# A retention layer with a gated feed-forward layer: tiles of one chunk of all batch entries, and a down projection as seven products of halves

## The chip, the cores and the metric

The kernel runs on one core of one Trainium2 chip. A core has TensorE (PE in the profile; its weight loads are shown apart, as PEld), VectorE (DVE), ScalarE (ACT), GpSimd (POOL), and SyncE (SP), which here only issues DMAs. PSUM, which TensorE writes to, has eight banks; SBUF holds everything else. The metric is the time of the launch on the device in microseconds (us); the figure for the kernel before is a median of three runs.

## The reference

Two layers follow one another. The first is a recurrence over 768 positions for 4 batch entries (B) and 8 heads (H) of size 64 (D), in float32:

```python
gamma = 1.0 - 2.0 ** (-5.0 - np.arange(H))
scale = 1.0 / np.sqrt(D)
for t in range(S):
    state = gamma[None, :, None, None] * state + np.einsum('bhd,bhe->bhde', k[:, :, t], v[:, :, t])
    y[:, :, t] = scale * np.einsum('bhd,bhde->bhe', q[:, :, t], state)
```

Its output, reordered to x of (B*S, H*D) = (3072, 512), goes through a gated feed-forward layer with 1536 hidden columns:

```python
gate = 1.0 / (1.0 + np.exp(-(x @ w_gate)))
val = x @ w_val
return (gate * val @ w_out).astype(np.float32)
```

## The kernel before

**Chunks.** The recurrence is computed by chunks of 128 positions: inside a chunk as masked products (scores of k against q, a causal mask, then a product with v), and across chunks through a state of 64x64 for each head. There are 24 chunks, six for each batch entry, and they are worked through batch entry by batch entry. The decay is put in by tables: v is multiplied by a table on the way in (`scale_v`, `tabv`), and the output by another on the way out (`y_out`, `taby`). So k and q are used as they are loaded, and a state must pass from a chunk to the next.

**Steps of a chunk.** `load_kq` and `load_v` bring a chunk's k and q as bf16 and v as float32 (three DMAs that GpSimd issues; those of chunk 0 are issued by SyncE). k and q are then transposed: for chunks 0 to 11 on TensorE (`transposes`, `transposes_early`, evicted by ScalarE), from chunk 12 on by DMA (`xbar`, on SyncE's queue). `scores` fills two PSUM banks, `masks` moves them to SBUF on VectorE, `inter` multiplies the state of the chunks before (`zbd`) with q, `intra` adds the chunk's own part, `y_out` writes the result, times its table, on VectorE into `xT`, the input of the feed-forward layer. `state`, `state_sum` and `casts` carry the state on. From chunk 4 on, two chunks at a time go through `block`.

**Tiles of the feed-forward layer.** Four chunks make one tile of 512 tokens, six tiles in all. For each of twelve groups of 128 hidden columns, `up` makes eight matmuls of 128x512 into two banks; ScalarE takes the sigmoid of one (`gs`), VectorE multiplies it with the other into `hT`. `up_columns` does the same for columns that become ready later. `down` takes twelve matmuls of 128x512 for each 128 tokens (48 for a tile), ScalarE copies the bank out, SyncE stores it. The last 128 tokens go through `last_down`, in three pieces of 256, 128 and 128 columns.

**Order.** The order on every engine is written out by hand (`manual_schedule`): a list of groups for each tile, in which a plan puts the attention steps between `up` and `down` groups. Each engine works its list in order. PSUM tiles are one bank each, seven banks in a pool named `ff` in the profile, and one for the state (`z`). Since TensorE works in order, a matmul whose input or bank isn't ready holds back all that follow. `keep_on` issues matmuls without a use in the first microseconds.

Of the kernel before, what the change touches and what calls it, by code (L numbers as in the profile page):

```python
# [17 lines left out]
def kernel(  # L18
# [15 lines left out]
    NCH = S // C  # L34
    NP = H // 2
    KT = D_MODEL // 128
    NFF = D_FF // 128
    scale = 1.0 / math.sqrt(D)
# [5 lines left out]
    ld = ctx.enter_context(tc.tile_pool(name="ld", bufs=12))  # L44
# [5 lines left out]

    NG = B * NCH
    NT = N_TOK // 512
    XBAR = 12
    qn, kn, vf = {}, {}, {}

    def src(x, g):
        b, c = divmod(g, NCH)
        return x[b, :, c * C:(c + 1) * C, :].rearrange("h s d -> s h d")

    def load_v(g, eng):  # L60
        vf[g] = ld.tile([C, H, D], F32, tag="vf", name="vf", bufs=8)
        eng.dma_start(out=vf[g], in_=src(v, g))  # L62

    def load_kq(g):
        kn[g] = ld.tile([C, H, D], BF16, tag="kn", name="kn")
        qn[g] = ld.tile([C, H, D], BF16, tag="qn", name="qn")
        nc.gpsimd.dma_start(out=kn[g], in_=src(k, g))  # L67
        nc.gpsimd.dma_start(out=qn[g], in_=src(q, g))  # L68

    def load_chunk(g):  # L70
        load_kq(g)
        load_v(g, nc.gpsimd)
# [16 lines left out]
    kf = const.tile([C, H, D], F32, name="kf")  # L89
    qf = const.tile([C, H, D], F32, name="qf")  # L90
    nc.sync.dma_start(out=kf, in_=src(k, 0))
    nc.sync.dma_start(out=qf, in_=src(q, 0))
    nc.scalar.preload_act_table(AX.Exp)
    load_v(0, nc.sync)
    tokv = const.tile([128, NCH], I32, name="tokv")
    nc.gpsimd.iota(tokv, pattern=[[C, NCH]], base=0, channel_multiplier=1)
    ident = const.tile([128, 128], BF16, name="ident")
    make_identity(nc, ident)
    toky = const.tile([128, 384], I32, name="toky")
    nc.gpsimd.iota(toky, pattern=[[1, 384]], base=0, channel_multiplier=0)  # L100
    load_chunk(1)
# [4 lines left out]
    load_chunk(2)  # L106

    tabv = const.tile([128, NCH, H], F32, name="tabv")
    for h in range(H):
        nc.scalar.activation(tabv[:, :, h], tokv, AX.Exp, scale=-lg[h])  # L110
    lgp = const.tile([128, NP], F32, name="lgp")
    lsc = const.tile([128, 1], F32, name="lsc")
    nc.vector.memset(lsc, math.log(scale))
    for p in range(NP):
        nc.vector.memset(lgp[0:D, p:p + 1], lg[2 * p])
        nc.vector.memset(lgp[D:128, p:p + 1], lg[2 * p + 1])
    gup = const.tile([128, NP], F32, name="gup")
    for h in range(H):
        nc.vector.memset(gup[h % 2 * D:(h % 2 + 1) * D, h // 2:h // 2 + 1], math.exp(384 * lg[h]))
    zbd = [const.tile([128, NP, C], BF16, name=f"zbd{i}") for i in range(4)]  # L120
    for t in zbd:
        nc.vector.memset(t, 0.0)
    taby = const.tile([128, NP, S], F32, name="taby")

    def make_taby(cols):
        for p in range(NP):
            nc.scalar.activation(taby[:, p, cols], toky[:, cols], AX.Exp, scale=lgp[:, p:p + 1], bias=lsc)

    def extend_taby(lo, hi):
        nc.gpsimd.tensor_tensor(taby[:, :, lo:hi], taby[:, :, lo - 384:hi - 384],  # L130
                                gup.unsqueeze(2).to_broadcast([128, NP, hi - lo]), op=ALU.mult)

    causal4 = causal.unsqueeze(1).to_broadcast([128, NP, 128])


    xT, vs, qkT, sc, stA, stB, y, zbds = {}, {}, {}, {}, {}, {}, {}, {}
    zz, za = {}, {}
# [4 lines left out]
    def pair(t, p):  # L142
        return t[:, 2 * p:2 * p + 2, :].rearrange("s h d -> s (h d)")

    def transposes(g):
        tp = bank([128, 2 * NP, C], BF16)
        for i, x in enumerate((kn[g], qn[g])):
            for p in range(NP):
                nc.tensor.transpose(tp[:, i * NP + p, :], pair(x, p), ident)  # L149
        qkT[g] = at.tile([128, 2 * NP, C], BF16, tag="qkT", name="qkT", bufs=6)  # L150
        nc.scalar.activation(qkT[g], tp, AX.Copy)  # L151

    def transposes_early(g):
        qkT[g] = at.tile([128, 2 * NP, C], BF16, tag="qkT", name="qkT", bufs=6)
        for i, x in enumerate((kn[g], qn[g])):
            tp = bank([128, NP, C], BF16)
            for p in range(NP):
                nc.tensor.transpose(tp[:, p, :], pair(x, p), ident)
            nc.scalar.activation(qkT[g][:, i * NP:(i + 1) * NP], tp, AX.Copy)

    def xbar(g):
        qkT[g] = ld.tile([128, 2 * NP, C], BF16, tag="qkX", name="qkX", bufs=8)
        for i, x in enumerate((kn[g], qn[g])):
            nc.sync.dma_start_transpose(out=qkT[g][:, i * NP:(i + 1) * NP, :],
                                        in_=x.rearrange("s h d -> s (h d)"))

    def scale_v(g, eng):
        vs[g] = ld.tile([C, H, D], BF16, tag="vs", name="vs", bufs=8)
        eng.tensor_tensor(vs[g], vf[g], tabv[:, g % NCH, :].unsqueeze(2).to_broadcast([C, H, D]),  # L169
                          op=ALU.mult)  # L170

    def scores(g):
        t = qkT[g]
        sc[g] = (bank([128, NP, C]), bank([128, NP, C]))
        for p in range(NP):
            for i in range(2):
                half = slice(i * D, (i + 1) * D)
                nc.tensor.matmul(sc[g][i][:, p, :], t[half, p, :], t[half, NP + p, :], start=True, stop=True)  # L178

    def masks(g):  # L180
        stA[g] = at.tile([128, NP, C], BF16, tag="stA", name="stA", bufs=4)
        stB[g] = at.tile([128, NP, C], BF16, tag="stB", name="stB", bufs=4)
        nc.vector.tensor_tensor(stA[g], sc[g][0], causal4, op=ALU.mult)  # L183
        nc.vector.tensor_tensor(stB[g], sc[g][1], causal4, op=ALU.mult)  # L184

    def inter(g):
        y[g] = bank([128, NP, C])
        if g % NCH > 0:
            for p in range(NP):
                nc.tensor.matmul(y[g][:, p, :], zbd[(g - 1) % 4][:, p, :], qkT[g][:, NP + p, :],  # L190
                                 start=(p == 0), stop=False, skip_group_check=True)

    def state(g, to, start, stop=True):
        for p in range(NP):
            for i in range(2):
                nc.tensor.matmul(to[i * D:(i + 1) * D, p, :], kn[g][:, 2 * p + i, :], vs[g][:, 2 * p + i, :],  # L196
                                 start=start, stop=stop, skip_group_check=True)

    def state_out(g, z):
        for i in range(2):  # L200
            half = slice(i * D, (i + 1) * D)
            nc.scalar.copy(zbd[g % 4][half, :, half], z[half])  # L202

    def state_early(g):
        if g == 0:
            zz[0] = pz.tile([128, 2, NP, D], F32, tag="z", name="z")
# [7 lines left out]
    def new_za(g):  # L214
        za[g] = at.tile([128, NP, D], F32, tag="za", name="za", bufs=3)
        return za[g]
# [285 lines left out]
```

## Time and profile before

| | |
|---|---|
| median of three runs | 233.92 us (233.79 to 234.39) |
| the profiled execution: span from the first to the last instruction | 232.9 us |
| its own device time | not given apart from its span; the median lies 1.0 us above the span |
| TensorE clock granted | 1.000 of full speed over the whole span |
| busy: PE, DVE, ACT, POOL | 222.9, 110.0, 91.8, 92.2 us |
| DMA, from 6 to 116 us of the span | busy nine tenths or more of every slice |
| HBM read, written | 28.31 MB, 6.29 MB |

Busy time of PE is the time in which any matmul is in flight, so it says that there are no gaps, and not that each matmul is fast. In a row of a group, "xcount" is how many instructions are in it, "mean ns of one" is the length of one from start to end; matmuls overlap, so what a matmul costs in a row of matmuls is the distance of their starts, which the chain of waits and the timeline show.

### The profile page before, as it was taken

The numbers are of one execution on the slowest core, as the hardware profiler recorded it, in microseconds if no ns is written. First come the engines' busy times: TensorE is split into PE (matmuls) and PEld (weight loads), VectorE is DVE, ScalarE is ACT, GpSimd is POOL, SyncE is SP. The second block draws the span as 40 slices with busy tenths as digits, with TensorE's granted clock in tenths as the row PEclk, the third lists the DMA queues.
The fourth block names the chain that finished last, engine by engine and source line by source line (L and its number), as shares of the span: only waits on it lengthen the run. The fifth ranks groups of instructions, "written<-read, shape, count | busy, mean of one in ns | idle before, by whom it ended". The sixth has DMA issues, their size and how long they took to land.

```text
span 232.9 us, 4448 instructions
## 1 busy us (share of the span) xinstructions
PE 222.9 (96%) x1781; PEld 125.5 (54%) x1802; DVE 110.0 (47%) x201; ACT 91.8 (39%) x177; POOL 92.2 (40%) x111
## 2 busy tenths in 40 slices
PE   6878999999999999999999999999999999999994
PEld 5654644557889645445445445445445454444444
DVE  4465533275996562284924445716236711244301
ACT  8765233354727332253522432522532422433221
POOL 8999864788899743495118200000000000000000
PEclk9999999999999999999999999999999999999999
DMA  7999999999999999999959953001200011100022
GB/s 135 187 188 173 197 202 204 183 234 231 215 175 155 114 114 125 276 180 143 107 70 160 205 101 61 1 30 63 91 0 3 0 45 69 69 0 0 0 93 90
DMA packets 77557, 27.29 MB, mean 117 GB/s; under 512 B 65057, under 2 KB 73121, under 8 KB 77537
## 3 DMA queue, kind: packets, MB, share of 16 engines
q0 software_dynamic: 57616, 16.78, 75.9%
q1 hardware_dynamic: 19776, 10.16, 22.2%
q8 instruction: 14, 0.23, 0.4%
q10 hardware_dynamic: 144, 0.07, 0.1%
q14 instruction: 7, 0.05, 0.1%
HBM read 28.31 MB, written 6.29 MB: 149 GB/s over the span
## 4 chain that ended last, share of the span: by engine, by line
PE 84%; POOL 6%; DMA 3%; issue 2%; DVE 2%; ACT 1%; POOLq 0%
PE ff L285 46%; PE ff L316 25%; PE ff L299 5%; DMA wv<-in_moe_w_val_dram 3%; PE ff L237 2%; PE ff L178 2%; PE ff L190 2%; PE ff L149 1%; PE ff L336 1%; POOL qn L68 1%; POOL kn L67 1%; PE z L196 1%; POOL vf L62 1%; POOL vs L169 1%; POOL wg L81 1%
## 5 line engine op out<-in xcount | busy, mean ns | idle before, releaser
L290 DVE TENSOR_TENSOR hT<-gs,ff 128x512 bf16<-128x512 f32 (+2 forms) x72 | 45.6, 641 | 69.4 <-PE ff L285 57.1
L285 PE MATMUL ff<-xT,wg 128*128 128x512 bf16 (+2 forms) x277 | 68.0, 361 | 1.4 <-DVE xT L245 0.7
L285 PE MATMUL ff<-xT,wv 128*128 128x512 bf16 (+2 forms) x287 | 68.6, 361 | 0.7 <-DMA wv<-in_moe_w_val_dram 0.6
L289 ACT ACTIVATE gs<-ff 128x512 f32<-128x512 f32 (+2 forms) x72 | 40.2, 562 | 68.0 <-PE ff L285 62.0
L316 PE MATMUL ff<-wo,hT 128*128 128x512 bf16 x267 | 61.1, 379 | 0.9 <-issue 0.5
L285 PEld LDWEIGHTS <-wv 128*128 128x128 bf16 x288 | 28.1, 98 | 29.8 <-DMA wv<-in_moe_w_val_dram 0.9
L316 PEld LDWEIGHTS <-hT 128*128 128x128 bf16 x276 | 26.3, 98 | 31.3 <-DVE hT L290 0.6
L285 PEld LDWEIGHTS <-wg 128*128 128x128 bf16 x288 | 27.1, 98 | 28.5 <-issue 0.7
L321 ACT COPY ob<-ff 128x512 f32<-128x512 f32 x23 | 13.5, 585 | 51.1 <-PE ff L316 38.2
L245 DVE TENSOR_TENSOR xT<-ff,taby 128x512 bf16<-128x512 f32 x24 | 15.6, 686 | 25.9 <-PE ff L237 25.9
L169 POOL TENSOR_TENSOR vs<-vf,tabv 128x512 bf16<-128x512 f32 x14 | 14.7, 1060 | 26.0 <-DMA vf<-in_v_dram 22.9
L62 POOL DMA_DIRECT2D vf<-in_v_dram x23 | 20.8, 904 | 8.1 <-DMA kn<-in_k_dram 2.8
L67 POOL DMA_DIRECT2D kn<-in_k_dram x23 | 21.0, 912 | 3.2 <-DMA wo<-in_moe_w_out_dram 1.1
L68 POOL DMA_DIRECT2D qn<-in_q_dram x23 | 20.5, 892 | 3.1 <-DMA wo<-in_moe_w_out_dram 2.2
L183 DVE TENSOR_TENSOR stA<-ff,causal 128x512 bf16<-128x512 f32 x24 | 16.3, 681 | 2.7 <-PE ff L178 2.6
L184 DVE TENSOR_TENSOR stB<-ff,causal 128x512 bf16<-128x512 f32 x24 | 16.3, 679 | 0.0
L202 ACT CAST zbd<-za 64x256 bf16<-64x256 f32 x32 | 12.9, 403 | 8.6 <-DVE za L224 8.0
L169 DVE TENSOR_TENSOR vs<-vf,tabv 128x512 bf16<-128x512 f32 x10 | 7.3, 734 | 5.0 <-DMA vf<-in_v_dram 4.9
L151 ACT ACTIVATE qkT<-ff 128x1024 bf16<-128x1024 bf16 x8 | 8.2, 1026 | 1.6 <-PE ff L149 1.6
L328 PE MATMUL ff<-ident 128*128 128x128 bf16 x82 | 7.3, 254 | 1.6 <-POOL ident masks.py:199 1.6
L237 PE MATMUL ff<-stB,vs 128*64 128x128 bf16 x96 | 7.9, 222 | 0.4 <-DVE stB L184 0.4
L237 PE MATMUL ff<-stA,vs 128*64 128x128 bf16 x96 | 8.1, 222 | 0.0
(62 smaller groups left out, 141.5 us busy)
## 6 DMA issues: line engine op xcount, KB each, us to landing
vf<-in_v_dram POOLq DMA_DIRECT2D x23, 256.0 KB, 8.0
out_dram<-ob SPq DMA_DIRECT2D x23, 256.0 KB, 3.1
kn<-in_k_dram POOLq DMA_DIRECT2D x23, 128.0 KB, 7.8
qn<-in_q_dram POOLq DMA_DIRECT2D x23, 128.0 KB, 8.0
wg<-in_moe_w_gate_dram POOLq DMA_DIRECT2D x6, 256.0 KB, 7.5
wv<-in_moe_w_val_dram POOLq DMA_DIRECT2D x6, 256.0 KB, 8.0
wo<-in_moe_w_out_dram POOLq DMA_DIRECT2D x4, 384.0 KB, 11.4
kf<-in_k_dram SPq DMA_DIRECT2D x1, 256.0 KB, 3.4
```

The lines of the kernel that those rows point to most:

```text
L62: eng.dma_start(out=vf[g], in_=src(v, g))
L67: nc.gpsimd.dma_start(out=kn[g], in_=src(k, g))
L68: nc.gpsimd.dma_start(out=qn[g], in_=src(q, g))
L169: eng.tensor_tensor(vs[g], vf[g], tabv[:, g % NCH, :].unsqueeze(2).to_broadcast([C, H, D]), op=ALU.mult)
L183: nc.vector.tensor_tensor(stA[g], sc[g][0], causal4, op=ALU.mult)
L184: nc.vector.tensor_tensor(stB[g], sc[g][1], causal4, op=ALU.mult)
L237: nc.tensor.matmul(y[g][i * D:(i + 1) * D, p, :], vs[g][:, 2 * p + i, :], st[:, p, :], start=(first and p == 0), stop=True, skip_group_che ...
L245: nc.vector.tensor_tensor(xT[g // 4][:, :, col:col + C], y[g], taby[:, :, c * C:(c + 1) * C], op=ALU.mult)
L285: nc.tensor.matmul(u[:, lo:hi], w[:, kk, n1 * 128:(n1 + 1) * 128], xT[t][:, kk, lo:hi], start=(kk == 0), stop=(kk == KT - 1))
L289: nc.scalar.activation(gs[:, lo:hi], ps[0][:, lo:hi], AX.Sigmoid)
L290: nc.vector.tensor_tensor(hT[t][:, n1, lo:hi], gs[:, lo:hi], ps[1][:, lo:hi], op=ALU.mult)
L316: nc.tensor.matmul(o, hT[t][:, n1, sm * 128:(sm + 1) * 128], wo[:, n1, :], start=(n1 == 0), stop=(n1 == NFF - 1))
```

## The change

A tile is now made of the same chunk of all four batch entries: tile t holds positions 128t to 128t+127 of entries 0 to 3. Its loads and attention steps go by pairs P of batch entries (two pairs for a tile, 12 in all), each load twice as large as before. Tile 0 needs no state, and a state passes from tile to tile. The rows of the output that a tile writes are scattered accordingly.

The decay goes into k and q ahead of the transposes (`scaled`: k by a growing, q by a falling table): for pairs 2 and 3 on VectorE, from pair 4 on on GpSimd, from float32 loads. v is loaded as bf16 and used as it is. For pairs 0 and 1 the decay is in the mask (`mask0`). With that, `y_out` is a copy, and stands on ScalarE. Transposes are on TensorE for pairs 0 to 3, by DMA from pair 4 on.

The down projection of a tile is split into halves of its rows, of its hidden columns and of its output columns. Seven products of halves replace eight (a scheme by Strassen and Winograd): `hidden_sums` makes three new sums of halves of `hT` and overwrites one half by a fourth, `weight_sums` makes four from `wo` once, `product` accumulates six matmuls of 128x256 for each of seven products and two row groups (84 in place of 48 matmuls of 128x512 for a tile), and `fast_out` adds what is left to add on ScalarE and VectorE, and stores. Products of a tile stand among the `up` groups of the next (`ORDER`, one string for a tile, where u, a and b are `up` and its halves, X and Y products of the two row groups, a minus means the tile before, S and W the sums, K, Q, k, q the scalings on GpSimd and VectorE, L loads, J transposes by DMA, T on TensorE, F, B, E, Z and O attention steps).

The core of the diff:

```diff
+    def src(x, P):
+        t, j = divmod(P, 2)
+        return x[2 * j:2 * j + 2, :, t * C:(t + 1) * C, :].rearrange("b h s d -> s (b h) d")
+    def load(P, *what):
+        for n in what:
+            held, x = {"k": (kn, k), "q": (qn, q), "v": (vn, v)}[n]
+            if n == "v" or P < 4:
+                held[P] = ld.tile([C, 2 * H, D], BF16, tag=n, name=n + "n", bufs=4 if n == "v" else 3)
+            else:
+                held[P] = ld.tile([C, 2 * H, D], F32, tag=n + "f", name=n + "f", bufs=2)
+            nc.gpsimd.dma_start(out=held[P], in_=src(x, P))
...
+    def scaled(P, n, eng):
+        held, x, tab = {"k": (kt, kn, tabk), "q": (qt, qn, tabq)}[n]
+        held[P] = ld.tile([C, 2 * H, D], BF16, tag=n + "t", name=n + "t", bufs=3)
+        eng.tensor_tensor(held[P].rearrange("s (c h) d -> s c h d", c=2), x[P].rearrange("s (c h) d -> s c h d", c=2),
+                          tab[:, P // 2, :].unsqueeze(1).unsqueeze(3).to_broadcast([C, 2, H, D]), op=ALU.mult)
...
+    def y_out(P, c, eng):
...
+        if eng == "v":
+            nc.vector.tensor_copy(o, y[P, c])
+        else:
+            nc.scalar.copy(o, y[P, c])
...
+    def state_sum(P):
+        j = P % 2
+        if P < 2:
+            za[j] = const.tile([128, 2, NP, D], F32, name=f"za{j}")
+            nc.vector.tensor_copy(za[j], zz[P])
+        else:
+            nc.vector.tensor_tensor(za[j], za[j], zz[P], op=ALU.add)
...
+    def weight_sums(g):
...
+        nc.vector.tensor_tensor(wt[:, 0, fs], b12, b11, op=ALU.subtract)
+        nc.vector.tensor_tensor(t3, b22, b12, op=ALU.subtract)
+        nc.scalar.copy(wt[:, 2, fs], t3)
+        nc.vector.tensor_tensor(t2, t3, b11, op=ALU.add)
+        nc.scalar.copy(wt[:, 1, fs], t2)
+        nc.vector.tensor_tensor(wt[:, 3, fs], b21, t2, op=ALU.subtract)
...
+    def hidden_sums(t, g):
...
+        nc.vector.tensor_tensor(s1, a21, a22, op=ALU.add)
+        nc.vector.tensor_tensor(s2, s1, a11, op=ALU.subtract)
+        nc.vector.tensor_tensor(a21, a11, a21, op=ALU.subtract)
+        nc.vector.tensor_tensor(s4, a12, s2, op=ALU.subtract)
...
+    def product(t, i, n):
...
+        a, c = fast[i][0][:, :256], fast[i][0][:, 256:]
+        to = {1: a, 2: fast[i][1][:, :256], 3: c, 4: a, 5: c, 6: a, 7: a}[n]
+        for f in range(NFF // 2):
...
+            nc.tensor.matmul(to, left, right, start=(f == 0 and n in (1, 2)), stop=(f == NFF // 2 - 1),
+                             skip_group_check=True)
+    def fast_out(t, i, n):
...
+        if n == 5:
...
+            nc.scalar.copy(fast[i, "p"], a)
+            nc.vector.tensor_tensor(fast[i, "o"][0][:, :256], fast[i, "p"][:, :256], b[:, :256], op=ALU.add)
...
+        if n == 6:
+            nc.scalar.copy(p1, a[:, 256:])
+            nc.vector.tensor_tensor(lo[:, 256:], p1, a[:, :256], op=ALU.add)
+            nc.sync.dma_start(out=out[rows[0], :], in_=lo)
+        if n == 7:
+            nc.vector.tensor_tensor(hi[:, 256:], p5, a[:, :256], op=ALU.add)
+        if n == 4:
+            nc.scalar.copy(hi[:, :256], a[:, :256])
+            nc.sync.dma_start(out=out[rows[1], :], in_=hi)
...
-    def down(t, sm, part):
...
-        for n1 in range(part * half, (part + 1) * half):
-            nc.tensor.matmul(o, hT[t][:, n1, sm * 128:(sm + 1) * 128], wo[:, n1, :],
-                             start=(n1 == 0), stop=(n1 == NFF - 1))
...
+    up_half(0, 0, 0)
+    y_step(1, 0, "a")
+    up_half(0, 2, 0)
+    y_step(1, 1, "a")
+    up_half(0, 0, 1)
+    up_half(0, 2, 1)
+    load(3, "k", "q", "v")
+    for s in range(4):
+        load_out(s)
...
+    ORDER = [
+        "u4 k0 Z0 u5 k1 u6 Z1 k2 q2 u7 T2 S0 u8 F2 u9 S1 u10 L4 E2 u11 S2",
+        "a0 O2 a2 k3 q3 L5 a4 T3 a6 F3 K4 Q4 J4 a8 E3 O3 b0 W0 b2 W1 b4 W2 -X1 -X2 b6 -X5 L6 S0 b8 -X3 -X6 F4 u10 -X7 S1 -X4 K5 Q5 J5 u11 B5 O4 "
+        "-Y1 -Y2 S2 -Y5 K6 Q6 J6 L7 -Y3 -Y6 -Y7 -Y4 B6 O5",
+        "u0 u1 -X1 -X2 u2 -X5 u3 -X3 -X6 u4 -X7 -Y1 -Y2 K7 Q7 J7 L8 u5 -X4 -Y5 u6 -Y3 -Y6 B7 O6 u7 S0 -Y7 L9 K8 Q8 J8 u8 -Y4 S1 u9 B8 O7 u10 u11 S2",
...
+        "-X1 -X2 u0 -X5 u1 -X3 -X6 u2 -X7 -Y1 -Y2 u3 -X4 -Y5 u4 -Y3 -Y6 u5 -Y7 u6 -Y4 u7 S0 u8 S1 u9 u10 u11 S2 "
+        "X1 X2 Y1 Y2 X5 Y5 X3 X6 Y3 Y6 X7 Y7 X4 Y4",
+    ]
```

## The prediction

> **What bounds the kernel now.** First the page's head and its parts 1 and 4: where does the time go, and what does the chain of waits consist of?
>
> ```profile
> span 232.9 us, 4448 instructions
> PE 222.9 (96%) x1781; PEld 125.5 (54%) x1802; DVE 110.0 (47%) x201; ACT 91.8 (39%) x177; POOL 92.2 (40%) x111
> PE 84%; POOL 6%; DMA 3%; issue 2%; DVE 2%; ACT 1%; POOLq 0%
> ```
>
> TensorE is the path; loads are it only at the start. When it takes over, the timeline says; what each kind of matmul costs, the chain in order of time (start, length, what):
>
> ```profile
> 22.32 0.82 PE L285 MATMUL ff<-xT,wv 128*128 128x384 bf16 x4 [0.56 <-DMA wv<-in_moe_w_val_dram]
> ...
> 26.95 10.74 PE ff L285 x49
> 40.50 2.59 PE ff L316 x12
> 43.09 0.45 PE ff L149 x8
> 57.30 0.55 PE ff L178 x16
> 57.85 0.37 PE z L196 x16
> 67.72 3.49 PE ff L299 x32
> 79.08 0.45 PE ff L190 x8
> ```
>
> At 22.32 the last late load ends, and from 26.95 (the fifth `up` group) matmuls follow without a gap to the last one's end at 229.85. A 128x512 costs 2.59/12 = 0.216 us, a 128x256 with its own weights 3.49/32 = 0.109, so half; an `up` group 8 x 0.216 = 1.73. For two chunks: scores 0.55, inter 0.45, state 0.35, intra 0.475 (distance of starts), and 0.45 for the transposes of one.
>
> Work before from 26.95: 68 `up` groups 117.7, 288 `down` matmuls 62.3, transposes of 8 chunks 3.6, scores of 20 5.5, inter of 17 3.8, intra of 20 4.75, state of 16 2.8: 200.5. The stretch is 202.9, so only 2.4 us is waiting. That is the measure for the new order.
>
> VectorE is at 47%, but on the new path. Its prices, and one collision:
>
> ```profile
> 71.40 2.06 POOL L169 TENSOR_TENSOR vs<-vf,tabv 128x512 bf16<-128x512 f32 x2
> ...
> 72.89 1.12 DVE L169 TENSOR_TENSOR vs<-vf,tabv 128x512 bf16<-128x512 f32 x1
> ...
> 84.06 0.41 DVE L224 TENSOR_TENSOR za<-za,z 128x256 f32<-128x256 f32 x1
> 145.29 0.68 DVE L184 TENSOR_TENSOR stB<-ff,causal 128x512 bf16<-128x512 f32 x1
> 145.88 0.68 DVE L183 TENSOR_TENSOR stA<-ff,causal 128x512 bf16<-128x512 f32 x1
> ```
>
> Read: a 128x512 takes 0.68, and 0.60 from start to start in a row; a 128x256 0.41; the scaling of v, with two inputs from SBUF, 0.69 elsewhere, took 1.12 beside GpSimd's scaling.
>
> **The change, part by part.** TensorE's work from the fifth group on: `up` the same, 117.7; products 504 x 0.109 = 55.1 (-7.2); transposes of pairs 2 and 3 1.8 (-1.8); inter of 10 pairs 4.5 (+0.7), state of 10 3.5 (+0.7), scores and intra as before. Sum 192.8: 7.7 us less.
>
> *The start.* The path is the fourth slice of weights in line (wv of columns 256 to 511). Landings follow one another by 1.3 us for such a load, 0.85 for 1024 rows cast to bf16, 1.15 for a 256 KB float32. Ahead of it and with it: before 6 x 1.15 + 6 x 0.85 + 4 x 1.3 = 17.2 and a landing at 22.3; after, four float32 loads (two each on SP and ACT) and k, q, v of pair 1, v of pair 0, 4 x 1.15 + 8 x 0.85 + 5.2 = 16.6: 21.7. Then half a group 0.9, a `y_step` and its copy on ACT 1.1, two half groups 3.5: the fifth group starts at 27.0, as before. Bounds: 25.2 if the copies on ACT set it, 29 if the four loads get in each other's way.
>
> *New waits in tile 0 and 1*, followed queue by queue with those prices. A 128x1024 scaling on VectorE is 1.2 (0.41 for 256, 0.69 for 512, so 0.27 for each 256 more). `hidden_sums` has four bf16 operations in a chain; no row has bf16 from SBUF on both sides. Bounds 0.41 (same bytes as the 128x256 float32 row) and 0.69 (same elements); I take 0.41, the row nearest in bytes, 1.6 a group, and keep 0.69 for the range.
>
> - "u4 k0 Z0 u5": state 0 needs the scaled k, behind hT of u4: u4's end + 0.8 + 1.2, TensorE idle 2.0, with u5 queued behind it. Z1 has u6 in between: 0.3.
> - "k2 q2 u7 T2": two scalings come after hT of u6 and the copy of the state; the transposes wait 0.3 and 1.05. T3 likewise 0.2 and 0.85.
> - "F3 a8 E3 O3 b0": masks (four in 2.4) end 0.4 after intra asks, then b0 needs both copies into xT: 1.2 more.
> - Three W groups (four operations and two copies) and S0 fall in a stretch of b groups of 1.73; with its hT a group costs VectorE 2.2. It is behind, so X4 (after X7, without a group between) waits 1.5 for the add that reads its bank, queued behind four masks, state and hT.
> - The seven Y products run in a row: Y3 waits for the copy of the bank, 1.15, Y7 for copy and add, 0.8, Y4 0.55. Then u0 of tile 2 for xT: 0.9.
>
> Sum 11.2. Later tiles have a group between dependent products, so I count only X1's last matmul, which waits for hT of u11 behind masks and S groups: 0.6, 0.6, 0.2, 0.35 at the ends of tiles 2 to 5. Waits 12.95 in all, against 2.4.
>
> *The end.* Before, from the last matmul to the span's end 3.05 (copy, a 64 KB store of 1.6 to landing). After: ACT copies 128x256 (0.39, a row of the sigmoid), then 256 KB, 3.1 to landing, with another just ahead (0.4), and the same 1.0 after it: 5.0.
>
> *At nothing, with the cover named:* `y_out` on ACT (24 x 0.59) lies beside `up`, ACT being idle three fifths; where `up` waits for it (b0 and u0 above) it is counted. `fast_out`'s 36 adds (0.41) and copies likewise. SP: 16 transposes of twice the size for 24, est. 1.2 to 2.5 us each of issue, with stores queued behind; J4 to J6 get their input when GpSimd has scaled (float32 loads of 1.15 each half, after `wo`, which lands at about 50): J4 lands at 62 to 66, wanted at 73; J5 70 to 79, wanted 80; J6 75 to 92, wanted 89. Price if late: up to 3. GpSimd: 16 scalings of 2.1 (two of its 1.04 rows) for 14 of 1.04, and 34 loads that at 0.9 to 1.8 each cost at most what 69 cost (62 us); its idle half covers them.
>
> Sum: 27.0 + 192.8 + 12.95 + 5.0 = 237.7 span, against 232.9. The medians lie 1.0 above the span: **238.7 us**.
>
> **Two rules of the Trainium skill.** The collision above (1.12 for 0.69, beside GpSimd) is a general one by "GPSIMD Engine Reference", section "8. Key points": GpSimd shares its SBUF interfaces with VectorE, and a VectorE operation with two SBUF inputs contends. It speaks against the change, which gives VectorE 84 such operations in the two kinds of sums and six scalings, and GpSimd 33 us of scalings. In its favour stands "VectorE: DVE Perf Modes", section "The perf-mode tier table": `tensor_tensor` on bf16 in SBUF runs at twice the float32 rate, which would settle the sums at the 0.41 end; no row here shows it.
>
> By rows: K4 to Q6 hold GpSimd 12.6 us in the stretch in which VectorE is late. Nothing of it may collide, or a third (4 us of VectorE on the path). I take nothing, as only one of the ten scalings on VectorE was hit.
>
> **The rivals.**
>
> *Faster, by fewer waits in tiles 0 and 1.* It decides at waits of 8.2 in place of 12.95: below that the 7.7 win. For it: four scalings make 4.2 of the waits (k0, k2, q2, q3), and would make less if bf16 input shortens them; the W groups are late by little; and the start may be at 25.2. Against: these are chains of rows, each in order on its engine, and the matmul behind them waits for the last. With half the waits and an early start 238.7 - 6.5 - 1.8 = 230.4.
>
> *VectorE becomes the bound.* Sums at 0.69: 1.1 us more for each of 18 S and 3 W groups; three S and W groups follow one another closely in tile 0 and 1, where I'd count 4 more, and in tiles 2 to 4 two S groups stand ahead of X1: 2 each. With 2 for collisions 238.7 + 12 = 251. For it the 1.12 row; against it 47% busy before, and the bytes.
>
> *Late transposes.* B5 or B6 wait for J5, J6, with the loads of pairs 5 and 6 slowed by transposes (before, by the list of DMA issues, loads issued at 68 to 78 us beside transposes took 10 to 18 us to land, those at 50 to 60 some 8): 3 to 8 more, 242 to 247.
>
> *Short matmuls don't pay:* a weight load takes 0.098 of each 0.109. The L299 row has one load for each matmul, so this is answered; left out.
>
> **How the numbers follow.** Within 0.3% is about what a measurement here can't tell from no change. Waits as counted, or up to 4 off either way: 0.48, 234.5 to 243. Fewer waits: 0.27, of which a tenth or so stays within 0.3%. VectorE the bound: 0.15. Late transposes: 0.10. Faster 0.26, same 0.04, slower 0.70. Range: the low end takes in half the waits gone with the start as before or a little better (230), the high end late transposes and half of VectorE's case (248).
>
> **What would show it.** Right: PE's chain has 128x256 products at 0.109; a gap of about 2 us after u4 ended by a scaling on VectorE, others at T2, T3, b0, X4 and Y3 to Y4, and X waits of half a microsecond later; VectorE and not a load is the releaser. The sums take 0.41 to 0.45. Wrong: gaps under 8 us between the fifth group and the end (then faster), sums of 0.69, waits on transposed q or k, or a fifth group that starts far from 27.

## The result, and the profile after

The changed kernel takes 270.1 us (median of four executions, 265.7 to 273.0) against 234.1 (233.8 to 234.4): 1.143 times as long, interval 1.135 to 1.151. The forecast was 238.7, range 230 to 248. Executions of one kernel spread by up to 5%, mostly with a lower mean clock in the slower ones; medians are over all of them, ratios and intervals over the faster ones. The profiled execution took 265.74 us, span 264.0. So of the 31.4 us between forecast and median 26.3 lie in the span, which is explained below; 0.7 are that a time lies 1.7 above its span and not 1.0; and 4.4 are that the profiled execution is the fastest of the four.

The head of the page, its parts 1, 2 (the clock) and 4, of the changed kernel:

```profile
span 264.0 us, 4709 instructions
PE 224.4 (85%) x1916; PEld 148.7 (56%) x1916; DVE 151.7 (57%) x265; ACT 101.7 (39%) x194; POOL 83.7 (32%) x77
PEclk9999999976998885899999999999999999999999
PE 71%; DVE 12%; DMA 7%; ACT 5%; issue 2%; SPq 1%; DVEq 0%; ACTq 0%
```

TensorE is idle 15% of the span instead of 4%, and its granted clock, full throughout before, falls in the 9th and 10th slice (53 to 66 us) and from the 13th to the 17th (79 to 112). The waits show in the timeline of TensorE; the bracket gives the idle time ahead of an instruction and what ended it:

```profile
26.95 1.03 PE L263 MATMUL ff<-xT,wg 128*128 128x512 bf16 x4
...
30.82 0.44 PE L211 MATMUL z<-vn,kt 128*64 128x64 bf16 x16 [1.99 <-DVE kt L164]
...
55.37 0.62 PE L149 MATMUL ff<-ident,kt 128*128 128x128 bf16 x8 [1.15 <-DVE kt L164]
58.22 1.03 PE L149 MATMUL ff<-ident,qt 128*128 128x128 bf16 x8 [2.22 <-DVE qt L164]
...
79.12 0.38 PE L338 MATMUL ff<-wt,hs 128*128 128x256 bf16 x2 [2.42 <-DVE wt L295]
83.78 1.26 PE L338 MATMUL ff<-wo,hs 128*128 128x256 bf16 x6 [2.53 <-ACT p L347]
...
102.50 1.04 PE L172 MATMUL ff<-qkT 64*128 64x128 bf16 x16 [8.36 <-DMA qkT<-qt]
...
157.19 0.39 PE L338 MATMUL ff<-wt,hs 128*128 128x256 bf16 x2 [2.11 <-DVE hs L312]
```

The fifth `up` group starts at 26.95, as forecast (27.0). The worst wait, 8.36 us, is for the transposed q of pair 5. All waits from there to the end, beside the forecast's items:

| wait | forecast | measured |
|---|---|---|
| first state ("u4 k0 Z0 u5") | 2.0 | 1.99 |
| second state, transposes of pair 2 | 0.3 + 1.35 | 0.98 + 0.51 |
| transposes of pair 3 | 1.05 | 3.37 |
| b0 for xT | 1.6 | 0.94 |
| stretch of W groups, X5, X3, X4 | 1.5 | 5.89 |
| pair 5's scores (J5) | 0 | 8.36 |
| Y3, Y7, Y4 | 2.5 | 2.10 |
| u0 of tile 2 | 0.9 | 0.69 |
| later tiles (forecast for other waits, see below) | 1.75 | 3.98 |
| sum | 12.95 | 28.8 |

In the later tiles, the wait that was forecast, X1's last matmul for hT, does not show in the timeline. The 3.98 are 2.11 for a sum of hidden values (157.19), 0.89 for an add and 0.58 for a multiply into hT that free a bank, and 0.40 for the transposed q of pair 8.

How long TensorE was at work, and at which clock, is told by the windows (columns: length; then busy time of PE, PEld, DVE, ACT, POOL, with counts; granted clock; DMA share; GB/s):

```profile
26.95:260.40 233.45, 204.24 (x1722) 132.46 (x1719) 140.59 (x245) 86.24 (x154) 64.69 (x47) 0.96 0.72 105
56.68:63.51 6.83, 5.29 (x40) 3.87 (x40) 2.81 (x4) 1.97 (x3) 6.83 (x6) 0.50 1.54 156
83.99:87.40 3.41, 3.41 (x35) 2.30 (x34) 2.98 (x8) 0.61 (x2) 0.30 (x1) 0.50 1.06 233
97.64:107.88 10.24, 5.38 (x63) 4.28 (x64) 4.51 (x9) 2.19 (x4) 2.94 (x3) 0.50 0.81 150
```

Of the 233.45 us from the fifth group to the last matmul's end TensorE was idle 29.2 (forecast 12.95) and busy 204.2 (forecast 192.8). The granted clock was 0.50 in the three stretches shown and 1.00 in all the rest of this window. Matmuls of 128x256 start every 0.213 us in these stretches, and every 0.109 elsewhere. TensorE was busy 14.1 us in them, so half of that, 7.0 us, is what the low clock cost. Run e14 below has 1.2 us more of matmuls to do; there the same part of the kernel, at full clock, reads:

```profile
27.06:229.16 202.10, 197.58 (x1686) 125.22 (x1683) 126.10 (x225) 85.43 (x151) 64.17 (x47) 1.00 0.79 121
```

So this work takes 197.6 - 1.2 = 196.4 at full clock, and the forecast's sum of work was 3.6 short: in e14, counted from start to start, `inter` and `intra` take 11.4 together (forecast 9.25), and the rest is spread over `up`, the down projection and state. Another 0.8 us of busy time stays unexplained. The tail took 3.6, not 5.0. In sum 237.7 + 16.3 (idle) + 3.6 (work) + 7.0 (clock) + 0.8 - 1.4 = 264.0.

**Why J5 was late.** SP's own queue (columns: start, length, what it issued):

```profile
57.10 3.90 SPq L158 DMA_TRANSPOSE qkT<-qt  x1
87.21 0.36 SPq L354 DMA_DIRECT2D out_dram<-ob  x1
92.40 0.35 SPq L359 DMA_DIRECT2D out_dram<-ob  x1
92.86 1.44 SPq L158 DMA_TRANSPOSE qkT<-kt  x1
94.40 3.29 SPq L158 DMA_TRANSPOSE qkT<-qt  x1
```

GpSimd had k and q of pair 5 scaled at 64.3. SP issued nothing from 61.0 to 87.2: first in its queue stood the store of X6's result (L354), then that of X4 (L359), and the transposes behind them. Each store went when its data was there, the first after an add on VectorE, the second after a copy on ScalarE:

```profile
86.76 0.42 DVE L353 TENSOR_TENSOR ob<-p,ff 128x256 f32<-128x256 f32 x1 [0.39 <-ACT p L352]
92.00 0.37 ACT L358 COPY ob<-ff 128x256 f32<-128x256 f32 x1 [2.67 <-PE ff L338]
```

The copy had waited for the product X4 on TensorE. So the transposes of tile 1 waited for the down projection of tile 0, as it stood in the order.

**Why VectorE was late.** Its timeline, and GpSimd's beside it:

```profile
53.19 2.13 DVE L164 TENSOR_TENSOR kt<-kn,tabk 128x1024 bf16<-128x1024 bf16 x1
55.24 2.92 DVE L164 TENSOR_TENSOR qt<-qn,tabq 128x1024 bf16<-128x1024 bf16 x1
77.50 1.57 DVE L295 TENSOR_TENSOR wt<-wo 128x512 bf16<-128x512 bf16 x1
78.99 2.38 DVE L296 TENSOR_TENSOR t<-wo 128x512 f32<-128x512 bf16 x1
152.43 4.70 DVE L312 TENSOR_TENSOR hs<-hT 128x512 bf16<-128x512 bf16 x1
```

```profile
151.23 1.90 POOL L164 TENSOR_TENSOR qt<-qf,tabq 128x1024 bf16<-128x1024 f32 x1
153.09 1.89 POOL L164 TENSOR_TENSOR kt<-kf,tabk 128x1024 bf16<-128x1024 f32 x1
154.95 1.89 POOL L164 TENSOR_TENSOR qt<-qf,tabq 128x1024 bf16<-128x1024 f32 x1
```

Undisturbed, these five take 1.22, 1.22, 0.42, 0.69 and 0.42 us. The last, ready at 152.4, ended at 157.1, 0.3 after the last of GpSimd's scalings in a row: it had waited out three of them. Six operations of this execution were hit, with an excess of about 10 us in all. Operations with one input in PSUM (the products into hT, masks, adds into ob) kept their times beside GpSimd.

### The profile page after: what moved, and what is told of

Its sections match the earlier page's. It is cut to its first block, busy times and chain, and to the rows that moved or that the text cites. A ratio compares the mean times of both kernels' runs of the same rounds, so it can differ in the third digit from the quotient of the medians.

```text
span 264.0 us, 4709 instructions
## 1 busy us (share of the span) xinstructions
PE 224.4 (85%) x1916; PEld 148.7 (56%) x1916; DVE 151.7 (57%) x265; ACT 101.7 (39%) x194; POOL 83.7 (32%) x77
## 4 chain that ended last, share of the span: by engine, by line
PE 71%; DVE 12%; DMA 7%; ACT 5%; issue 2%; SPq 1%; DVEq 0%; ACTq 0%
PE ff L263 33%; PE ff L338 20%; PE ff L279 9%; DMA qkT<-qt 6%; PE ff L172 3%; PE ff L192 2%; DVE hs L312 2%; DMA raw<-in_k_dram 2%; DVE qt L164 2%; DVE hT L268 2%; ACT xT L204 1%; DVE kt L164 1%; PE ff L149 1%; DVE st L179 1%; PE ff L186 1%
## 5 line engine op out<-in xcount | busy, mean ns | idle before, releaser
L268 DVE TENSOR_TENSOR hT<-gs,ff 128x512 bf16<-128x512 f32 x58 | 39.8, 686 | 47.0 <-PE ff L263 43.6
L263 PE MATMUL ff<-xT,wg 128*128 128x512 bf16 x232 | 59.6, 379 | 1.3 <-ACT xT L204 0.7
L263 PE MATMUL ff<-xT,wv 128*128 128x512 bf16 x232 | 59.5, 379 | 0.0
L267 ACT ACTIVATE gs<-ff 128x512 f32<-128x512 f32 x58 | 34.6, 597 | 53.5 <-PE ff L263 51.9
L179 DVE TENSOR_TENSOR st<-ff,causal 128x512 bf16<-128x512 f32 x40 | 24.8, 683 | 12.1 <-PE ff L172 12.1
L338 PEld LDWEIGHTS <-hs 128*128 128x128 bf16 x216 | 21.7, 101 | 14.3 <-issue 6.3
L338 PE MATMUL ff<-wt,hs 128*128 128x256 bf16 x144 | 20.7, 281 | 4.5 <-DVE wt L295 2.4
L338 PE MATMUL ff<-wt,hT 128*128 128x256 bf16 x144 | 19.3, 272 | 3.5 <-DVE ob L356 2.3
L338 PE MATMUL ff<-wo,hT 128*128 128x256 bf16 x144 | 18.8, 285 | 0.0
L284 DVE TENSOR_TENSOR hT<-gs,ff 128x512 bf16<-128x512 f32 x14 | 9.6, 686 | 15.1 <-PE ff L279 13.7
L279 PE MATMUL ff<-xT,wg 128*128 128x256 bf16 x112 | 16.1, 292 | 1.8 <-ACT xT L204 1.6
## 6 DMA issues: line engine op xcount, KB each, us to landing
wv<-in_moe_w_val_dram POOLq DMA_DIRECT2D x6, 256.0 KB, 11.4
```

The lines of the kernel that those rows point to most:

```text
L179: nc.vector.tensor_tensor(s, sc[P, c][i], mask0[:, i] if P < 2 else causal4, op=ALU.mult)
L263: nc.tensor.matmul(u[:, lo:hi], w[:, kk, n1 * 128:(n1 + 1) * 128], xT[t][:, kk, lo:hi], start=(kk == 0), stop=(kk == KT - 1))
L267: nc.scalar.activation(gs[:, lo:hi], ps[0][:, lo:hi], AX.Sigmoid)
L268: nc.vector.tensor_tensor(hT[t][:, n1, lo:hi], gs[:, lo:hi], ps[1][:, lo:hi], op=ALU.mult)
L279: nc.tensor.matmul(u[:, i], w[:, kk, (n1 + i) * 128:(n1 + i + 1) * 128], xT[t][:, kk, lo:lo + 256], start=(kk == 0), stop=(kk == KT - 1))
L284: nc.vector.tensor_tensor(hT[t][:, n1:n1 + 2, lo:lo + 256], gs, ps[1], op=ALU.mult)
```

## The experiments

Theories: **SP's order** (J5 behind stores), **collisions** (VectorE waiting out GpSimd's scalings), **the clock** (what a gap costs beyond itself), and, as rivals, that the data or the transposing loads are late in any order, and that tile 0's products are too much for the stretch in which they stand.

### e1: transposes ahead of stores

```diff
-... b6 -X5 L6 S0 b8 -X3 -X6 F4 u10 -X7 S1 -X4 K5 Q5 J5 u11 B5 O4 -Y1 -Y2 S2 -Y5 K6 Q6 J6 L7 -Y3 ...
+... b6 -X5 L6 K5 Q5 J5 S0 b8 K6 Q6 J6 -X3 -X6 F4 u10 -X7 S1 -X4 u11 B5 O4 -Y1 -Y2 S2 -Y5 L7 -Y3 ...
-u0 u1 -X1 -X2 u2 -X5 u3 ... -Y2 K7 Q7 J7 L8 u5 -X4 -Y5 u6 -Y3 -Y6 B7 O6 u7 S0 -Y7 L9 K8 Q8 J8 u8 ...
+u0 u1 -X1 -X2 u2 -X5 K7 Q7 J7 L8 u3 ... -Y2 u5 -X4 -Y5 K8 Q8 J8 L9 u6 -Y3 -Y6 B7 O6 u7 S0 -Y7 u8 ...
```

> Only the order in which work is issued changes: the scalings and the transposing loads of pairs 5 and 6 (tile 1) and of pairs 7 and 8 (tile 2) are issued before the stores that follow the sixth product, so that they stand ahead of them in SP's queue. Theory 'SP's order' (the transposes J5 and J8 were late because a store ahead of them in SP's queue waited for the copy of its result, until 92.4 and 137.2 us, while their input was ready at 64.3 for J5): both gaps of TensorE, 9.7 us at 92.8 and 7.8 us at 138.8, shrink to at most 3 us, so 12 to 17 us go, and if the low clock after a gap costs what the windows make me estimate, another 4 to 8: 246 to 254 us. Rival 'the data are late' (GpSimd's loads and scalings, or the transposes themselves at 8 us, set the end): the gaps stay within 3 us of what they are, 264 us or more.

Measured: 255.0 us (251.3 to 256.4), ratio 1.075, 1.061 to 1.089; 15 us less. Profiled span 249.5; TensorE waits on no transposed q or k any more, and J5's two issues stand at 61.9 and 67.0, while GpSimd's scalings of pair 5 end at 63.7, as before (64.3). The clock is at half for 6.8 us in place of 20.5. So SP's order is shown as the cause of the longest wait, and the rival falls. Half of the expectation was a misreading: the chain of the changed kernel names a DMA from 139.08 for 7.4 us (J8), but TensorE's timeline has matmuls through all but 0.40 of it. The chain follows what landed last, and is no measure of idle time.

### e2 and e3: no scaling from pair 4 on

```diff
+            if P >= 4: held[P] = x[P]; return        # in scaled(); loads of all pairs cast to bf16
```

> Leaves out the decay factors of k and q from pair 4 on: GpSimd's scalings are gone and the loads come in bf16 straight away; the order of SP's queue is as in the changed kernel. Theory 'collisions' (operations on VectorE with two inputs in SBUF wait out a scaling on GpSimd; the excess over undisturbed ones adds up to about 10 us, not all of it on the path): 5 to 10 us go, the adds at 55, 77, 79 and 152 us take 0.4 to 1.3 us like their likes, and the two gaps behind SP's queue stay, each shorter by 1 to 3 us since the stores' copies come sooner: 256 to 265 us. Theory 'SP's order alone': under 3 us go, 267 us or more.

> Both edits at once: transposes of pairs 5 to 8 issued ahead of the stores, and no decay factors on k and q from pair 4 on (left out). If the two causes are separate, the gains of the two add, and what is left is the waits that were predicted and the low clock they bring: 238 to 246 us. If SP's order is all of it, no more than 2 us under the run with the order alone. If something else makes TensorE late in tiles 1 and 2, it stays above 250 us.

Measured: e2 251.0 us (ratio 1.069, 1.060 to 1.079), e3 244.2 (1.040, 1.032 to 1.047). Both leave the decay out from pair 4 on, so they compute something else. TensorE's waits in e2:

```profile
55.94 0.62 PE L149 MATMUL ff<-ident,qt 128*128 128x128 bf16 x8 [0.51 <-DVE qt L167]
73.19 0.38 PE L341 MATMUL ff<-wt,hs 128*128 128x256 bf16 x2 [1.26 <-DVE wt L298]
76.15 0.82 PE L341 MATMUL ff<-wo,hs 128*128 128x256 bf16 x6 [0.82 <-ACT p L350]
83.04 0.81 PE L341 MATMUL ff<-wt,hT 128*128 128x256 bf16 x6 [2.01 <-DVE ob L359]
89.62 1.03 PE L175 MATMUL ff<-qkT 64*128 64x128 bf16 x16 [3.59 <-DMA qkT<-qn]
```

The wait at the transposes of pair 3 falls from 3.37 to 0.51, those in the W stretch from 5.89 to 4.09 (X4's even grows, from 0.94 to 2.01), that of 2.11 at 157 is gone, and the one for J5 is 3.6. The gain is more than expected, since the stores ahead of J5 went out 8 us earlier and a transposing load landed in 3.3 us (median, from the DMA issues between 50 and 150 us) instead of 5.9 to 7.4. J5's ran while hardly a load was under way (one landed at 85.9, the next was issued at 92.1; in the changed kernel, two of 512 KB were, from 91.5 to 102.2). It is not the smaller loads as such: in e3, with the same ones, the medians are 6.5 and 8.2. So the run shows that GpSimd's scalings cost time by collisions, but not how much is theirs alone; e14 asks that again. By the faster executions the gains are 15 and 16 us, and e3's is 23: they don't add up, as they share the wait for J5. e3's profiled span is 241.9 against the forecast's 237.7, with TensorE idle 14.3 us (forecast 12.95): without the two mechanisms the forecast's sum is right to 2%, though not item by item, since the W stretch still takes 4.1 us for 1.5.

### e4: TensorE kept busy in the gaps

```diff
+        if done is not None and new in (5, 8):
+            keep_on(150 if new == 5 else 110)      # in block(), ahead of the scores
```

> Small matmuls on zeros are added ahead of the scores of tile 1's pair 5 and tile 2's pair 8, so that TensorE is busy through most of the two long gaps; the waits themselves stay, and nothing is reordered. Theory 'the clock': the granted clock stays near 1.0 in the 15 us after each of the two gaps, in which it was 0.5 for 4 and 9 us of windows; the part of the loss that is the clock and not the wait goes, 3 to 8 us: 262 to 267 us. Rival 'the low clock lies in stretches where TensorE waits anyway': within 1.5 us of the changed kernel's 270.

Measured: 272.3 us (268.6 to 282.3), no gain. It settles little: there was no second gap to fill, and there the fill itself stood on the path, as the chain shows:

```profile
148.03 6.14 PE ff L372 x110
```

In the first gap the wait shrank to 2.9 us, but pair 5's q landed 3 us later. The execution with the highest mean clock, 0.994, took 268.6 us, so what a higher clock gave back, the fill can have taken. What the low clock costs is thus known from the account above (7.0 us), which no run tests by itself, and from the spread: the four executions of the changed kernel had mean clocks of 0.961, 0.955, 0.948 and 0.923 and took 265.7, 269.2, 271.1 and 273.0 us.

### e6: tile 0's scalings earlier

```diff
+    scaled(0, "k", nc.vector)      # after up_half(0, 0, 0)
+    scaled(1, "k", nc.vector)      # after y_step(1, 1, "a")
-u4 k0 Z0 u5 k1 u6 Z1 k2 q2 u7 T2 ...
+u4 Z0 u5 k2 q2 u6 Z1 u7 T2 ...
```

> Only tile 0's scalings move: k of pairs 0 and 1 before the fourth and fifth up group, k and q of pair 2 one group earlier. The predicted waits of 2.0 us at the first state, 0.3 at the second and 1.4 at the transposes of pair 2 should go, 3 to 4 us; the two long gaps behind SP's queue stay. If these waits are on the path: 265 to 268 us, and TensorE's fifth group is followed without a gap of 2 us. If something behind them (the weights that land at 27, VectorE's backlog) takes their place: 269 us or more.

Measured: 269.0 us (264.2 to 272.1), within the spread. The waits of 1.99, 0.98 and 0.51 are gone, and one of 2.50 has come: pair 2's scores wait for copies of its transposes on ACT, which are queued behind copies of the state. A wait removed showed what was late next.

### e7: the down projection of before, transposes ahead

```diff
-            product(t, i, n); fast_out(t, i, n)
+            down(t, sm, part)        # 48 matmuls of 128x512 a tile, in the places of products 2, 5, 6, 7
-    hidden_sums, weight_sums
```

> The earlier transposes, and in place of the seven products the down projection of before (48 matmuls of 128x512 for a tile), so no sums of hidden values or of weights and no adds of results; everything else of the change stays. TensorE gets 7.2 us more to do. Theory 'VectorE's extra work and its collisions are what the products cost': the wait of some 10 us in the stretch with the weight sums, the collided sum of 4.7 us and the 5 us of results that wait for one another go, against 7.2 us of matmuls, and the tail gets 1 to 2 us shorter: 238 to 245 us, below the 255 us of the run with earlier transposes alone. Rival 'the products are a gain that other parts of the change eat up': 258 us or more.

Measured: 250.1 us (245.4 to 256.7), ratio 1.052, 1.048 to 1.057: 5 to 6 us below e1 with 7.2 us more of matmuls, so sums, collisions with sums, chained results and the waits that they bring cost some 12 to 14 there. In the profiled execution, the longest of the five (256.7), scores wait 5.2 and 2.7 us for transposes again, in two places; whether these waits also keep the shorter ones (245.4 and more) from the forecast's 245 no profile shows.

### e9 and e10: tile 0 by the old down projection, all scalings on VectorE

```diff
-        "K": lambda t, P: scaled(P, "k", nc.gpsimd), ...
+        # pairs 4 to 11 by "k", "q" (VectorE), all loads cast to bf16; "D": the down projection of before
+"u4 Z0 u5 k2 q2 u6 Z1 u7 T2 u8 F2 u9 k3 q3 u10 L4 E2 u11",
+"a0 O2 a2 T3 L5 a4 F3 a6 E3 O3 a8 k4 q4 J4 b0 b2 -D0 b4 -D1 k5 q5 J5 b6 -D2 L6 b8 -D3 F4 S0 W0 u10 -D4 u11 k6 q6 J6 -D5 S1 W1 B5 O4 "
+"-D6 L7 S2 W2 B6 O5 -D7",
...
```

(e10: in the last tile, too, D0 to D7 in place of sums and products.)

> Four things at once, to see what the change is worth when the causes found are taken away: the scalings of pairs 4 to 11 go to VectorE (1.2 us each, from bf16 loads, so GpSimd computes nothing beside it), tile 0's are early as in the run above, tile 0's down projection is that of before (so no sums fall into the crowded stretch, and the weight sums come a tile later), and transposes are issued ahead of stores. By the terms of the prediction: 27.0 to the fifth group, matmuls 192.8 + 1.2, tail 5.0 and 1.0 around the span are 227.0, and the waits decide. If collisions and SP's order were the whole of the unpredicted loss, waits are 4 to 9 us: 231 to 236 us, about the kernel before. If VectorE, with 20 us of scalings more, becomes the bound: above 240 us.

> As the run above, with the last tile's down projection too as before: 1.2 us more of matmuls, a tail 2 us shorter (a copy of 128x512 and a store behind the last of 12 matmuls, where now seven products end together with copies and adds), and three groups of sums less. 0.5 to 2.5 us below the run above: 229.5 to 235 us. If the tail is set by the store alone, within 0.7 us of it.

Measured: e9 254.9 us (1.081, 1.074 to 1.088), e10 255.0 (1.090, 1.087 to 1.092). Neither is what was expected. e9's waits, the longest (columns: what waited for what, us in total, times, longest):

```profile
PE ff L169 <- DMA qkT<-qt: 10.1, 4, 4.7
PE ff L183 <- ACT xT L201: 4.3, 1, 4.3
PE ff L169 <- ACT qkT L150: 3.6, 2, 2.5
```

The transposes were issued ahead of the stores, but too late: the load behind the wait of 4.6 us, at 93.4, took 9.0 us to land, in a stretch in which loads keep the DMA engines full, and the one behind the wait of 4.7, at 167.6, took 3.1, but was issued at 164.4 only, behind its scaling on VectorE. And ACT stood still for 5 us at the head of its queue, at a cast of the weight sums that waited for VectorE, with the results of a block behind it. GpSimd computes nothing here: collisions were not the whole of it. The old down projection at the end gained nothing: from the last `up` groups on, e10's end takes 14.2 us and e9's 13.5.

### e11 and e12: the order spread out

The diff is against e9; the last tiles likewise have k and q apart.

```diff
+        "z": lambda t, P: (state(P), state_sum(P)),
+"u4 z0 u5 k2 u6 q2 z1 u7 T2 O0 u8 k3 u9 F2 u10 q3 O1 L4 E2 u11",
+"a0 O2 a2 T3 L5 a4 F3 k4 q4 J4 a6 E3 O3 W0 a8 b0 W1 b2 -D0 b4 k5 q5 J5 -D1 W2 b6 -D2 L6 b8 k6 q6 J6 -D3 F4 S0 u10 -D4 u11 -D5 B5 O4 S1 "
+"-D6 L7 B6 O5 S2 -D7",
+"u0 k7 u1 -X1 q7 J7 -X2 u2 -X5 L8 u3 -X3 -X6 u4 -X7 -Y1 k8 -Y2 u5 q8 J8 -X4 -Y5 L9 u6 -Y3 -Y6 B7 O6 u7 S0 -Y7 u8 -Y4 S1 u9 B8 O7 u10 u11 S2",
...
```

(e12: "D" in all tiles, no S, W, X and Y.)

> As the run with tile 0's down projection as before (254.9 us), with the work of its order spread out: the scalings of k and q one by one between up groups, each pair's transposing loads issued 10 us or more ahead of the scores that want them, the weight sums from 58 us on, where VectorE is half idle and before ACT is asked for the results of blocks, and the copies of a state behind those of the transposes. In that run's trace TensorE waited 10.1 us for transposed q, 4.3 and 3.6 us for copies on ACT queued behind casts that waited for VectorE, and some 2 us elsewhere, and ran at a low clock after each. Theory 'order on the queues alone': these 18 us and their low clocks go, 230 to 238 us. Rival 'the transposing loads can't be on time, since the loads of later pairs hold the DMA engines': 245 us or more.

> As the run above, with the down projection of before in all tiles: no sums, adds or weight sums, 6.0 us more of matmuls (5 tiles x 1.2). If the products are worth their 7.2 us where they are given room, 3 to 7 us above the run above; if VectorE's sums and the results that wait for one another still cost more than that, it is below it.

Measured: e11 234.0 us (ratio 0.9992, 0.9971 to 1.0013), e12 239.1 (1.017, 1.010 to 1.024). e11's page and its longest waits after the start:

```profile
span 232.2 us, 4606 instructions
...
PEclk9999999999999999999999999999999999999998
```

```profile
PE ff L335 <- DVE ob L353: 0.9, 1, 0.9
PE ff L169 <- ACT qkT L150: 0.8, 1, 0.8
```

With the same work as e9, only ordered otherwise, some 19 us go (21 by the medians); no wait is over 1 us, the clock stays up, and the kernel stands where the one before stood. The rival that transposing loads can't be on time falls. e12 shows that the seven products are worth most of their price: it takes 4 to 5 us more than e11, where 6.0 were expected for five tiles. Its profile has 4.7 us more of matmuls at full clock, and 1.5 for a low clock beside a wait of 2.15 us for a transposed q; a start 0.8 us earlier and fewer other waits take some of it back.

### e13 and e15: fewer waits yet

```diff
-... O3 W0 a8 ... -D3 F4 S0 u10 -D4 u11 -D5 B5 O4 S1 -D6 L7 B6 O5 S2 -D7
+... O3 W0 a8 ... -D3 F4 u10 -D4 u11 -D5 B5 O4 S0 -D6 L7 B6 O5 S1 -D7
-... u5 q8 J8 -X4 ... u7 S0 -Y7 u8 -Y4 S1 u9 ...
+... u5 S0 -X4 ... u7 -Y7 u8 S1 -Y4 u9 ...
```

> As the spread-out run (234.0 us, its profiled execution 7 us of waits or less between the fifth group and the end), with the groups of hidden sums moved away from masks and from the adds that free a bank: the first group of a tile three up groups earlier, the second behind the eighth group, and tile 0's scores of pair 2 ahead of the copies of the state. The waits of 0.9, 0.6, 0.5, 0.6, 0.8 and 0.6 us that the trace shows there should go: 2 to 3.5 us less, 230.5 to 232 us. If VectorE is so full that each of them comes back elsewhere, within 1 us of 234.

> As the run with fewer waits (232.9 us), in which a state was copied out only after the next pair's part had been added to it, so that one pair read a wrong state; here the copy stands before that sum, behind tile 0's ninth up group. Same matmuls and sums otherwise: within 0.7 us of 232.9, so 0.2 to 0.7% below the kernel before. If the copies on ACT now hold up the transposes of pair 2: 233.5 to 234.5 us.

Measured: e13 232.9 us (ratio 0.9943, 0.9921 to 0.9965), e15 234.9 (0.9979, 0.9944 to 1.0013). e13 copied a state after the next sum, so it computes something else; e15 does not, and its interval holds no change. No version is shown to be faster than the kernel before.

### e14: GpSimd's scalings back in the spread order

```diff
-k4 q4 ... k11 q11      # VectorE, from bf16 loads
+K4 Q4 ... K11 Q11      # GpSimd, from float32 loads
```

> The spread-out run with its 16 scalings of pairs 4 to 11 back on GpSimd, from float32 loads as in the changed kernel; the order is the same otherwise. VectorE has 19.5 us less to do (16 x 1.22). Theory 'collisions': VectorE's operations with both inputs in SBUF (sums, weight sums, scalings) that meet one of GpSimd's 16 operations of 1.9 us wait them out, and GpSimd's loads queue behind its scalings: 4 to 12 us slower than 234 in spite of the smaller load on VectorE, with single sums of 1 to 4 us in the trace. Rival 'VectorE's load matters, not the collisions': 234 us or less.

Measured: 236.2 us (233.6 to 240.6), ratio 1.0039, 1.0008 to 1.0069, at most 1% above e11. Six operations met a scaling, these two for longest:

```profile
58.77 2.27 DVE L300 TENSOR_TENSOR wt<-wo,t 128x512 bf16<-128x512 bf16 x1
84.75 2.12 DVE L315 TENSOR_TENSOR hs<-hT,hs 128x512 bf16<-128x512 bf16 x1
```

They take 0.69 and 0.42 undisturbed, so 3.3 us in excess; all six have 4.9, half of the changed kernel's 10. So collisions cost little here, where they are fewer and VectorE has slack; the 4 to 12 us expected was too much. In the changed kernel they fell into the stretch in which TensorE and ACT waited for VectorE.

### e16: the changed kernel, ordered otherwise

```diff
+"u4 z0 u5 k2 u6 q2 z1 u7 T2 O0 u8 S0 k3 u9 F2 u10 S1 q3 O1 L4 E2 u11 S2",
+"a0 O2 a2 T3 L5 a4 F3 K4 Q4 J4 a6 E3 O3 W0 a8 b0 W1 b2 -X1 b4 K5 Q5 J5 -X2 W2 b6 L6 K6 Q6 J6 -X5 b8 -X3 -X6 F4 u10 -X7 -Y1 -Y2 u11 -X4 -Y5 B5 O4 S0 "
+"-Y3 -Y6 L7 B6 O5 -Y7 S1 -Y4 S2",
...
```

> The changed kernel with nothing but another order: seven products in all tiles, scalings of pairs 4 to 11 on GpSimd from float32 loads, tile 0's products and sums in the stretch of tile 1 as there; what moves is where scalings, transposing loads, weight sums, hidden sums and state copies stand, as in the spread-out runs. Theory 'order alone': 233 to 242 us; 1.2 us of matmuls less than the spread-out run with GpSimd's scalings (236.2 us), and tile 0's three groups of sums, 5 us on VectorE, and results that wait for one another back in tile 1. Rival 'tile 0's products in that stretch cost it, whatever the order': 246 us or more.

Measured: 247.5 us (243.8 to 248.0), ratio 1.056, 1.053 to 1.060: the median lies in the rival's range, the two shortest executions (243.8 and 245.95) between the two. Its longest waits after the start:

```profile
PE ff L338 <- DVE ob L356: 5.2, 2, 2.7
PE ff L338 <- DVE wt L295: 1.9, 1, 1.9
```

So of the 33 to 36 us lost, order alone gives back 20 to 23, and tile 0's products in that stretch cost 10 to 12 more than its old down projection (e16 against e14, the rest alike but for the places of its sums) in this order; both theories are right in part. Part of these 10 to 12 can be collisions again: VectorE's excess beside GpSimd is 10.3 us in e16 and 4.9 in e14, and no run has tile 0's products in this order without GpSimd's scalings. Whether a third order could hold them was not tried.

## Why the prediction was wrong

**Right.** The first state's wait (1.99 for 2.0); the hidden sums (0.42 us each for 0.41, where "VectorE: DVE Perf Modes" in the Trainium skill, section "The perf-mode tier table", spoke for the low end); products at 0.109 (twelve in 1.31) and most of their worth (e12); the waits at Y3 to Y4 and u0. The releaser is VectorE in most of the waits, as forecast. The tail was 1.4 us shorter.

**Right by luck.** The start (26.95 for 27.0; the terms given add up to 27.2). The path was said to be the weights, wv's second slice landing at 21.7. It landed at 20.5, and from the first half group at 17.6 on TensorE waited for no weights at all, only 0.68 us for a copy of `xT` on ScalarE. What the forecast had as a bound for this case, 25.2, was 1.7 too early.

**Wrong: "SP: ... with stores queued behind".** The prediction asked what the longer transposes hold up, and not what holds up the transposes. It gave J5's landing by when its input is ready (70 to 79) and put SP at nothing; in fact it was issued at 92.9 behind two stores and landed at 102.4. It cost 8.4 us of waiting where the sum had nothing, and with the low clock behind it and the other transposes that e1 moves 15 (e1). Waits on transposed q were among the prediction's own signs of being wrong. The rival "late transposes" had the place, but for another reason (slow loads), with a price of 3 to 8 and a chance of 0.10.

**Wrong: "I take nothing, as only one of the ten scalings on VectorE was hit".** The single row of 1.12 for 0.69 was read as a price of a third; it was a case of waiting, whose price is what is left of GpSimd's work: up to 4.3 us. The waits in the W stretch (5.89 us for 1.5), at pair 3 (3.37 for 1.05) and at 157 (2.11) fall by 1.8, 2.9 and 2.1 without the scalings (e2), so some 7 us of waits go with them. "SBUF — State Buffer" in the Trainium skill, section "SBUF: two separate sides", has it as a lock held for a whole instruction; the five rows above agree, and go further, since the operation at 152.4 waited for three in a row. But in e14, with half of the excess and VectorE not behind, collisions cost 1% at most.

**Too small: the W stretch itself.** "X4 ... waits 1.5" is 4.1 us in X5, X3 and X4 even without any scaling on GpSimd (e2): sums and results of tile 0's products are more than VectorE and ScalarE get done there. In another order these products cost 10 to 12 us more than the old down projection (e16 against e14).

**Not priced: the clock.** Before, it was full throughout, and the prediction gave none of its waits a consequence. Here it was 0.50 in the three stretches shown, and cost 7.0 us. The first began at 56.7, in the second of two waits of 1.15 and 2.22 us; a wait of 2.42 us ahead of 79.12 was not followed by one until 84.0. "TensorE: Matmul & The Clock Gate" in the Trainium skill, section "Part 1: The HAM clock gate", has the array fall to half rate after an idle window of some 3.4 us. The long gap agrees, the clock fell 3.5 us into it; the other two falls don't, as no wait ahead of them was longer than 2.53 us.

**The rivals.** "VectorE becomes the bound" (251 us, 0.15) and "late transposes" came together, with the clock on top. The range took them as alternatives, but they share a source: VectorE late in tile 1 delays the products whose stores SP's queue waits for. It is not the only one: in e2, with VectorE less late and the stores out 8 us earlier, 3.6 of the 8.4 us for J5 stay, as the order itself puts the transposes behind the stores.

## What to carry to other kernels

For every DMA that a change moves, list what stands ahead of it on its queue and when that gets its data, not only when its own input is ready; a store of another tile's result can hold a load for 28 us. When several engines wait for one in the same stretch, small excesses add up through their queues, and moving work to where that engine has slack (here some 19 us without a change in the work, e9 to e11) can be worth more than making a part cheaper (here 4 to 5 us for the products, e12). A gap on TensorE can cost more than its length: price the low clock behind it (here 7.0 us beside 29.2 of gaps).

## What was not expected of the hardware

- A VectorE operation with both inputs in SBUF waited out up to three GpSimd operations in a row (0.42 us became 4.70); operations with an input in PSUM took at most 0.02 us more beside GpSimd, in all runs.
- A transposing load of 128x1024 bf16 from SBUF landed 3.1 to 3.4 us after the start of its issue where few loads ran, and up to 20.8 after it where the DMA engines were full (pair 4's q in the changed kernel); SP's time to issue it rose from 1.3 to as much as 8.0 us (e1).
- The clock fell to half without a gap of 3.4 us: at 56.7, when TensorE had been busy for 1.57 of the 3.41 us before (waits of 1.15 us and the first 0.7 of the next). It came back after 6.8, 3.4 and 10.2 us.
